# Attention and two gated layers on one core: two weight conversions at a time beside attention, two tiles split ahead, the first down products later

## The chip, the cores and the metric

The program runs on one core of one Trainium2 chip. The metric is the device time of one execution in microseconds; the kernel before takes 1159.92 us, the median of three runs (1158.78 to 1161.83).

## The reference, cut to what matters

Attention over 4 batches, 12 heads, 448 positions and a head width of 64 feeds two dense layers over 1792 tokens of width 768. The attention weight is a sigmoid, not a softmax.

```python
scores = q @ k.T / sqrt(64) - log(448);  x = sigmoid(scores) @ v      # per batch and head
h = x @ w_in;  y = (h * cos(h)) @ w_out                               # layer 1, 768 -> 2048 -> 768
z = (silu(y @ w_gate) * (y @ w_val)) @ w_out2                         # layer 2, 768 -> 1536 -> 768
```

q, k and v are 32-bit floats. The five weight matrices arrive as 64-bit floats, and have to be turned into 32-bit ones on the chip.

## The kernel before, in words

**Precision.** Every product is made of three passes over pairs of high and low parts of the operands (`THREE`, line 176). A tile is "split" when ScalarE has copied its high part and VectorE has subtracted that from the whole to get the low part; `split` and `lower` in `operands()` (lines 400 to 419) do this for weights. A split weight tile lives in one slot of `pairs`.

**Stages.** First `attention()` (line 511): 24 pairs of heads, one after the other. For each pair, TensorE makes the scores of three blocks of 128 keys (line 559), then the weighted sums of the pair before (lines 583 and 586), then the scores of the 64 keys left over (line 571). ScalarE makes the sigmoids (line 549) and copies the high part of the weighted sum (line 615); VectorE splits q and k of the next pair (lines 538 to 546) and takes the low part of the weighted sum (the `lo` of line 616, recorded at line 530). That low part reads PSUM bank 7, which the next pair's weighted sums write. Then layer 1: 8 chunks of the width 2048, each for 4 groups of 448 tokens, 32 units in all; a unit is two up products (`up`, 18 matmuls each, line 863) and three down steps (`down`, 12 matmuls each, line 720) that `some(downs)` runs one at a time. Then layer 2: two halves of the tokens, six chunks each, the up products in a seven-product scheme (`seven`, line 809).

**Weight conversion.** There are 68 tiles of 768 KB. `conversions()` (line 299) loads one, runs one or two ScalarE and four or five VectorE instructions over it, stores 384 KB to a scratch in DRAM, and takes the next. During attention four such chains run, on four pieces of the result buffers R[0] and R[1] that attention does not need (`lent`, lines 211 to 214). From the fourth last pair on (line 620) a chain that ends its tile takes no further one. After attention two chains run on buffers of their own, and share one slot for the converted tile (`convs`).

**Reading the weights back.** `loads()` (line 363) brings converted tiles in order of need into a ring of three slots, and `operands()` splits them as `pairs` slots come free. One `pairs` slot exists during attention (`make_pairs(xp, 1, "a")`, line 224), and four more are made after it (line 911).

**Order of the work.** All is written out by a planner (class `Order`): each task asks for an engine and names a time, the planner starts the earliest that can start, and the lower rank wins a tie (up products 0, h cos h 3, weight splits 4, conversions 6). The chip then keeps that order on each engine. In attention the planner is told with `beside(...)` (line 469) how much of each 6.0 us pair slot attention itself takes: ScalarE 1.1 us of the first 2.0 and 3.3 of the other 4.0, VectorE the first 2.8, and the DMA issue queue of SP the first 2.0. Conversions get what is left.

```python
for i in range(2):                                   # tensor_engine(), layer 1, unit n
    yield from up(n, i, upbanks[next(turn) % 4])
    for _ in range(1 + i):                           # one down step of unit n - 1, then two
        yield from some(downs)
```

Of the kernel before, what the change touches and what calls it, by code (L numbers as in the profile page):

```python
# [9 lines left out]
F32 = mybir.dt.float32  # L10
# [139 lines left out]
def block_kernel(  # L150
# [12 lines left out]
    P = 128  # L163
    B, NP, D, _, _, S = qk.shape
# [21 lines left out]
    xp = ctx.enter_context(tc.tile_pool(name="xp", bufs=1))  # L186
# [5 lines left out]
    R = [xp.tile([P, 2, KD, N], F32, tag=f"r{h}", name=f"r{h}") for h in range(NH)]  # L192
# [16 lines left out]
        free_t.give(ring[:, a])  # L209

    WT, lent = KD * P, []
    for i in range(4):
        part = R[i // 2].rearrange("p j k n -> p (j k n)")[:, i % 2 * 3 * WT:(i % 2 + 1) * 3 * WT]
        lent.append((part[:, :2 * WT].bitcast(I32).rearrange("p (n two) -> p n two", two=2), part[:, 2 * WT:]))
    zero = R[1].rearrange("p j k n -> p (j k n)")[:, -S:].bitcast(mybir.dt.bfloat16)[:, :S]
    nlog = xp.tile([P, 1], F32, tag="nlog", name="nlog")
    warm = xp.tile([P, 1], F32, tag="warm", name="warm")
    pairs, singles, gslots, tmps, downbanks = (Slots(order) for _ in range(5))

    def make_pairs(pool, n, name):  # L220
        for i in range(n):
            pairs.give(pool.tile([P, 2, 2, KH, P], F32R, tag=f"w{name}{i}", name=f"w{name}{i}"))

    make_pairs(xp, 1, "a")
    for i in range(2):
        downbanks.give(4 + 2 * i)
    upbanks = [Slots(order) for _ in range(4)]
# [135 lines left out]
    def loads():  # L363
        for need in needs():
            t = yield free_t
            for w, f, i, k in need:
                there, event = scratch[id(w), f + i]
                yield event
                there = scratch[id(w), f + i][0]
                if k is None:  # L370
                    yield move(t, there)
                else:
                    yield move(t[:, i * W:(i + 1) * W], there[:, k * W:(k + 1) * W])
            arrived = order.event()
            arrivals.append((t, arrived))
            if waiting_load:
                waiting_load.pop(0).set()
            order.spawn(landed(arrived), 0)
# [101 lines left out]
    def inputs(h):  # L480

        b11, b12, b21, b22 = (R[h][:, j, k * KH:(k + 1) * KH] for k in range(2) for j in range(2))
        make = {
            1: (b11, None), 2: (b21, None), 5: (b11, (b12, b11)), 6: (b11, (b22, b11)),
            7: (b12, (b22, b12)), 4: (b21, (b21, b11)), 3: (b22, None),
        }

        def to_hi(out, t):
            def do(engine):
                if engine == "ACT":  # L490
                    nc.scalar.activation(out=out, in_=t, func=AF.Copy)
                else:
                    nc.vector.tensor_copy(out, t)
            return {"ACT": 1.55, "DVE": 1.2}, do

        yield source[h]
        for i in ORDER:
            yield x_left[h - 1, i] if h else x_used[PLACES[i][0]]
            t, parts = make[i]
            if parts:  # L500
                yield vec(1.6, t, parts[0], parts[1], SUB)
            hi, lo = X[i][:, :, 0], X[i][:, :, 1]
            yield to_hi(hi, t)
            yield vec(1.6, lo, t, f32(hi), SUB)
            x_ready[h, i].set()
# [193 lines left out]
    def down(n):  # L699

        layer, g, c = units[n]

        def weights(e, i):
            return ("d", c, i) if layer == 1 else ("d", n, i, e // KH)

        for j in range(2 if layer == 2 else 1):
            for i in range(2):
                yield g_ready[n, i, j]
            for d in range(0, KD, 2):
                first = yield downbanks  # L710
                for e in range(d, d + 2):
                    for i in range(2):
                        yield made_event(weights(e, i))

                def do(_, first=first, d=d, j=j):
                    for e in range(d, d + 2):
                        for i in range(2):
                            w, g = operand(weights(e, i)), gs[n, i, j]
                            for m, p in THREE:
                                nc.tensor.matmul(  # L720
                                    banks[:, first + e - d, :N],
                                    lhsT=w[:, m, e % KH if layer == 2 else e, :], rhs=g[:, p],
                                    start=(i, m, p) == (0, 0, 0), stop=(i, m) == (1, 1),
                                )

                yield {"PE": 12 * PRODUCT}, do
                for e in range(d, d + 2):
                    for i in range(2):
                        if e == KD - 1 and g == G - 1 if layer == 1 else j and e % KH == KH - 1:
                            give(weights(e, i))  # L730
                        if e == KD - 1:
                            gslots.give(gs.pop((n, i, j)))
                order.spawn(accumulate(n, j, d, first), 2)
                yield None
# [105 lines left out]
    def some(downs):  # L840

        got = None
        while True:
            try:
                want = downs.send(got)
            except StopIteration:
                return False
            if want is None:
                return True
            got = yield want  # L850

    def up(n, i, bank):

        _, g, c = units[n]
        out = yield bank
        yield made_event(("u", c, i))
        cols = slice(g % 2 * N, (g % 2 + 1) * N)

        def do(_):
            w, x = operand(("u", c, i)), X1[g // 2]  # L860
            for k in range(KD):
                for m, p in THREE:
                    nc.tensor.matmul(  # L863
                        out, lhsT=w[:, m, k, :], rhs=x[:, k, p, cols],
                        start=(k, m, p) == (0, 0, 0), stop=(k, m) == (KD - 1, 1),
                    )

        yield {"PE": 18 * PRODUCT}, do
        if g == G - 1:
            give(("u", c, i))  # L870
        if c == NF1 // 2 - 1 and i == 1 and g % 2:
            x_used[g // 2].set()
        order.spawn(h_cos_h((n, i, 0), out, lambda: bank.give(out)), 3)

    def tensor_engine():
        turn = itertools.count()
        downs = (want for want in ())
        for n in range(n_units):
            if n < n_first:
                for i in range(2):  # L880
                    yield from up(n, i, upbanks[next(turn) % 4])
                    for _ in range(1 + i):
                        yield from some(downs)
            else:
                if n == n_first:
                    while (yield from some(downs)):
                        pass
                z = {}
                for u in range(2):
                    yield from seven(n, u, next(turn), z, downs)  # L890
            downs = down(n)
        while (yield from some(downs)):
            pass

    with tc.manual_schedule():
        nc.gpsimd.memset(nlog, -math.log(S))
        for h in range(NH):
            order.spawn(inputs(h), 3.5)
        order.spawn(loads(), 3)
        order.spawn(operands(), 4)  # L900
        for raw, t in lent:
            returned.append(order.event())
            order.spawn(conversions(raw, t, returned[-1]), 6)
        attention()
        with tc.tile_pool(name="mp", bufs=1) as mp:
            for i in range(2):
                raws.give(mp.tile([P, WT, 2], I32, tag=f"raw{i}", name=f"raw{i}"))
                order.spawn(conversions(), 6)
            sum_room.append(mp.tile([P, W], F32, tag="sum", name="sum"))
            convs.give(mp.tile([P, WT], F32, tag="cv", name="cv"))  # L910
            make_pairs(mp, 4, "b")
            for i in range(4):
                gslots.give(mp.tile([P, 2, N], F32R, tag=f"g{i}", name=f"g{i}"))
            for i in range(3):
                tmps.give(mp.tile([P, 2, N], F32, tag=f"u{i}", name=f"u{i}"))
            order.spawn(tensor_engine(), 0)
            order.run()
            assert not order.open
# [51 lines left out]
```

## Time and profile before

| | us |
|---|---|
| median of three runs | 1159.92 |
| the profiled execution | 1162.79 |
| its span, first to last instruction | 1161.0 |
| attention, to the first up product | 168.98 |
| layer 1, to the last up product's end | 168.98 to 632.3 |
| layer 2 | 649.3 to 1161 |

Engines are named PE (TensorE), PEld (its weight loads), DVE (VectorE), ACT (ScalarE), POOL (GpSimd) and SP (which only issues DMAs here). A timeline row gives start, length, engine, source line, operation, output and inputs, count, and in brackets how long the engine stood idle before it and what ended that. Many conversions and splits are issued by helpers, so they carry the lines 233 (ScalarE), 236 (VectorE) and 242 (DMA); the tile names tell them apart: `r` and `raw` are conversion buffers, `cv` is a converted tile, `sw..` is a scratch in DRAM, `t` is a ring slot, `wa` and `wb` are split weights, `x` is the attention output. With the clock, 1.00 stands for TensorE's full speed.

### The profile page before, as it was taken

To read this page: it belongs to the slowest core of one execution; us is meant where nothing else is said; L and a number is where in the kernel's file an instruction comes from. 1 tells how busy PE (TensorE), PEld (TensorE's weight loads), DVE (VectorE), ACT (ScalarE), POOL (GpSimd) and SP (SyncE) were. 2 spreads that over 40 slices of the span, in tenths; PEclk is the share of its full clock that TensorE was granted. 3 is DMA by queue.
4 is the path that set the end of the run, shared out by engine and by line. 5 is a ranking of instruction groups with operands and counts; after the bars stand their busy time and mean duration, and the time that the engine had idled before them with its cause. 6 is when DMAs were issued, how large, how long until landed. Compare 5 with 4: busy or idle time off the path is not lost. (4 is left out here: it accounts for less than half of the span.)

```text
span 1161.0 us, 14377 instructions
## 1 busy us (share of the span) xinstructions
PE 1122.1 (97%) x5531; PEld 966.0 (83%) x5531; DVE 821.9 (71%) x1165; ACT 555.2 (48%) x837; POOL 80.6 (7%) x68
## 2 busy tenths in 40 slices
PE   8999989999999999999999889999998999999998
PEld 4445548999999999999998779999997899999997
DVE  5777756668787777777787977687469765557654
ACT  6677755654444444444444546454334344333430
POOL 0000000000000000000000311021021111112100
PEclk9999999999999999999999989999998999999999
DMA  9999934443333434343422254432210421121102
GB/s 272 255 278 284 275 123 159 138 142 117 131 128 123 136 115 143 109 150 110 150 102 76 68 182 158 149 124 82 69 55 28 133 92 62 55 68 55 41 15 95
DMA packets 51908, 146.42 MB, mean 126 GB/s; under 512 B 5760, under 2 KB 21120, under 8 KB 51840
## 3 DMA queue, kind: packets, MB, share of 16 engines
q1 hardware_dynamic: 51696, 145.28, 39.0%
q8 instruction: 43, 0.70, 0.3%
q10 hardware_dynamic: 144, 0.23, 0.1%
q14 instruction: 25, 0.20, 0.1%
HBM read 113.25 MB, written 32.24 MB: 125 GB/s over the span
## 5 line engine op out<-in xcount | busy, mean ns | idle before, releaser
L720 PE MATMUL banks<-g,wb 128*128 128x448 f32 x1512 | 340.7, 369 | 6.5 <-ACT g L233 3.5
L720 PEld LDWEIGHTS banks<-g,wb 128*128 128x128 f32 x1512 | 284.9, 189 | 34.9 <-ACT g L233 4.7
L236 DVE TENSOR_TENSOR r<-banks,r 128x896 f32<-128x896 f32 x144 | 157.0, 1091 | 126.0 <-PE banks L720 125.8
L809 PE MATMUL banks<-x,wb 128*128 128x448 f32 x864 | 188.0, 366 | 10.0 <-DVE x L236 4.6
L809 PEld LDWEIGHTS banks<-x,wb 128*128 128x128 f32 x864 | 162.5, 189 | 25.0 <-DVE x L236 5.2
L863 PE MATMUL banks<-x,wb 128*128 128x448 f32 x864 | 183.1, 365 | 0.0
L863 PEld LDWEIGHTS banks<-x,wb 128*128 128x128 f32 x864 | 162.9, 188 | 13.2
L233 ACT ACTIVATE g<-u 128x448 fp32r<-128x448 f32 x104 | 60.0, 577 | 142.8 <-DVE u L236 133.2
L233 ACT ACTIVATE u<-u 128x448 f32<-128x448 f32 x148 | 84.9, 576 | 81.0 <-DVE u L645 54.3
L233 ACT ACTIVATE u<-banks 128x448 f32<-128x448 f32 x104 | 56.2, 541 | 108.7 <-PE banks L863 65.8
L236 DVE TENSOR_TENSOR u<-u,banks 128x448 f32<-128x448 f32 x124 | 76.3, 616 | 43.9 <-PE banks L809 34.8
L720 PE MATMUL banks<-g,wa 128*128 128x448 f32 x360 | 88.5, 369 | 0.0
L236 DVE TENSOR_TENSOR wb<-t,wb 128x768 fp32r<-128x768 f32 x72 | 68.9, 966 | 19.9 <-ACT wb L233 19.3
L233 ACT ACTIVATE wb<-t 128x768 fp32r<-128x768 f32 x72 | 59.8, 840 | 46.5 <-PE banks L809 12.8
L236 DVE TENSOR_TENSOR g<-u,g 128x448 fp32r<-128x448 f32 x104 | 68.4, 660 | 18.0 <-ACT g L233 18.0
L809 PE MATMUL banks<-x,x 128*128 128x448 f32 x315 | 73.8, 384 | 4.1 <-DVE x L236 3.7
L583 PE MATMUL banks<-a,vs 128*64 128x448 f32 x288 | 63.3, 577 | 10.8 <-DVE x L530 10.8
L720 PEld LDWEIGHTS banks<-g,wa 128*128 128x128 f32 x360 | 68.3, 190 | 6.3
L809 PEld LDWEIGHTS banks<-x,x 128*128 128x128 f32 x315 | 62.0, 199 | 12.1 <-DVE x L236 4.1
L549 ACT ACTIVATE a<-banks,nlog 128x896 f32<-128x896 f32 x72 | 67.4, 1008 | 7.0 <-PE banks L559 6.8
L645 DVE SCALAR_TENSOR_TENSOR u<-u 128x448 f32<-128x448 f32 x64 | 39.8, 622 | 35.8 <-ACT u L233 35.7
L389 POOL TENSOR_TENSOR sum<-t 128x384 f32<-128x384 f32 x14 | 17.0, 1214 | 674.7 <-PE banks L720 577.9
(87 smaller groups left out, 1286.9 us busy)
## 6 DMA issues: line engine op xcount, KB each, us to landing
raw<-in_w_out SPq DMA_DIRECT2D x20, 768.0 KB, 4.6
raw<-in_qk SPq DMA_DIRECT2D x47, 224.0 KB, 9.5
raw<-in_w_gate SPq DMA_DIRECT2D x12, 768.0 KB, 4.7
raw<-in_w_val SPq DMA_DIRECT2D x12, 768.0 KB, 4.5
vs<-in_v SPq DMA_DIRECT2D x24, 320.0 KB, 8.0
r<-in_w_in SPq DMA_DIRECT2D x10, 768.0 KB, 9.3
t<-swg SPq DMA_DIRECT2D x19, 384.0 KB, 3.2
t<-swv SPq DMA_DIRECT2D x17, 384.0 KB, 3.0
```

The lines of the kernel that those rows point to most:

```text
L233: return {"ACT": time}, lambda _: nc.scalar.activation(**kw)
L236: return {"DVE": time}, lambda _: nc.vector.tensor_tensor(out=out, in0=in0, in1=in1, op=op)
L389: on.tensor_tensor(out=out, in0=a, in1=b, op=op)
L549: nc.scalar.activation(out=a, in_=sc, func=AF.Sigmoid, bias=nlog, scale=1.0 / math.sqrt(D))
L583: nc.tensor.matmul(o[half], lhsT=vw[:, 2 * c + j], rhs=a[:, j], start=c == 0, stop=False)
L645: yield {"DVE": 0.65}, lambda _: nc.vector.scalar_tensor_tensor(out=f, in0=f, scalar=MAGIC, in1=u, op0=ALU.subtract, op1=ALU.subtract)
L720: nc.tensor.matmul(banks[:, first + e - d, :N], lhsT=w[:, m, e % KH if layer == 2 else e, :], rhs=g[:, p], start=(i, m, p) == (0, 0, 0), s ...
L809: nc.tensor.matmul(bank, lhsT=w[:, m, k, :], rhs=x[:, k, p, :], start=(k, m, p) == (0, 0, 0) and i in (1, 5), stop=(k, m) == (KH - 1, 1), ...
L863: nc.tensor.matmul(out, lhsT=w[:, m, k, :], rhs=x[:, k, p, cols], start=(k, m, p) == (0, 0, 0), stop=(k, m) == (KD - 1, 1),)
```

## The change

Four edits. The chains beside attention are two instead of four, both in R[0]. The constant `nlog` and the small `warm` tile move into the tail of R[1]. Two of the five `pairs` slots now exist during attention, and three are made after it, so that two weight tiles can be split early. And in layer 1, for the units 0 and 1, all down steps stand behind the second up product: unit 0's three down steps then come after both up products of unit 1, not one of them between the two.

```diff
-    for i in range(4):
+    for i in range(2):
         part = R[i // 2].rearrange("p j k n -> p (j k n)")[:, i % 2 * 3 * WT:(i % 2 + 1) * 3 * WT]
         lent.append((part[:, :2 * WT].bitcast(I32).rearrange("p (n two) -> p n two", two=2), part[:, 2 * WT:]))
-    zero = R[1].rearrange("p j k n -> p (j k n)")[:, -S:].bitcast(mybir.dt.bfloat16)[:, :S]
-    nlog = xp.tile([P, 1], F32, tag="nlog", name="nlog")
-    warm = xp.tile([P, 1], F32, tag="warm", name="warm")
+    last = R[1].rearrange("p j k n -> p (j k n)")
+    zero = last[:, -S:].bitcast(mybir.dt.bfloat16)[:, :S]
+    nlog, warm = last[:, -S - 1:-S], last[:, -S - 2:-S - 1]
...
-    make_pairs(xp, 1, "a")
+    make_pairs(xp, 2, "a")
...
-                    for _ in range(1 + i):
+                    for _ in range(((1, 2) if n > 1 else (0, 3))[i]):
                         yield from some(downs)
...
-            make_pairs(mp, 4, "b")
+            make_pairs(mp, 3, "b")
```

## Rows read from the trace of the kernel before

**Rows 1.** The page's first part: busy us, share of the span, instructions.
```profile
PE 1122.1 (97%) x5531; PEld 966.0 (83%) x5531; DVE 821.9 (71%) x1165; ACT 555.2 (48%) x837; POOL 80.6 (7%) x68
```

**Rows 2.** Windows: length, busy by engine (instructions), granted clock, DMA share, GB/s.
```profile
8.00:150.00 142.00, 133.92 (x758) 72.27 (x756) 106.96 (x228) 105.47 (x134) 0.00 (x0) 0.97 0.94 273
150.00:160.00 10.00, 7.80 (x39) 3.60 (x37) 8.11 (x16) 4.72 (x7) 0.00 (x0) 0.83 0.30 118
...
300.00:400.00 100.00, 100.00 (x491) 91.86 (x491) 76.19 (x105) 45.92 (x75) 0.00 (x0) 1.00 0.39 133
...
632.32:700.00 67.68, 57.46 (x254) 50.50 (x253) 56.01 (x65) 33.94 (x49) 14.20 (x9) 0.92 0.35 117
700.00:860.00 160.00, 159.71 (x786) 147.05 (x785) 116.18 (x150) 72.50 (x114) 26.91 (x22) 1.00 0.34 107
```

**Rows 3.** Timeline of PE in attention: start, length, work, idle before.
```profile
10.18 1.20 PE L571 MATMUL banks<-q,kb 128*128 128x448 f32 x3
...
69.00 1.10 PE L571 MATMUL banks<-q,kb 128*128 128x448 f32 x3
...
74.97 1.11 PE L571 MATMUL banks<-q,kb 128*128 128x448 f32 x3
...
81.30 3.50 PE L583 MATMUL banks<-a,vs 128*64 128x448 f32 x12 [2.43 <-DVE x L530]
...
85.72 1.27 PE L571 MATMUL banks<-q,kb 128*128 128x448 f32 x3
...
164.26 1.11 PE L571 MATMUL banks<-q,kb 128*128 128x448 f32 x3
```

**Rows 4.** Timeline of DVE just before that stall.
```profile
75.31 0.36 DVE L538 CAST k<-raw 128x384 fp32r<-128x384 f32 x1 [3.72 <-DMA raw<-in_qk]
...
78.89 1.82 DVE L320 SCALAR_TENSOR_TENSOR r<-r 128x768 int32<-128x768 int32 x2
80.63 0.62 DVE L530 TENSOR_TENSOR x<-banks,x 128x448 fp32r<-128x448 f32 x1
```

**Rows 5.** Waits of DVE (20 to 160 us) and of SP's queue (0 to 200): total, times, longest.
```profile
DVE k L538 <- DMA raw<-in_qk: 22.4, 8, 3.8
...
SPq L242 <- DVE r L236: 57.3, 12, 8.9
```

**Rows 6.** DMA issues up to 165 us: all traffic; one kind, KB each, median us to landing.
```profile
DMA packets 16139, 41.84 MB, mean 254 GB/s; under 512 B 1791, under 2 KB 7935, under 8 KB 16127
...
raw<-in_qk SPq DMA_DIRECT2D x47, 224.0 KB, 9.5
```

**Rows 7.** Groups up to 169 us, two steps of a conversion: busy, mean ns | idle before.
```profile
L236 DVE CUSTOM_DVE_ANT_0 r<-r 128x1536 uint16<-128x1536 uint16 x18 | 16.9, 953 | 0.1
...
L317 DVE TENSOR_SCALAR r<-r 128x768 int32<-128x768 int32 x18 | 9.8, 553 | 0.0
```

**Rows 8.** Timeline of PE at the start of layer 1.
```profile
168.98 4.16 PE L863 MATMUL banks<-x,wa 128*128 128x448 f32 x18
...
182.86 0.47 PE L720 MATMUL banks<-g,wb 128*128 128x448 f32 x1 [1.83 <-ACT g L233]
...
196.07 3.80 PE L863 MATMUL banks<-x,wa 128*128 128x448 f32 x18
...
210.78 3.80 PE L863 MATMUL banks<-x,wa 128*128 128x448 f32 x18
...
225.49 3.80 PE L863 MATMUL banks<-x,wb 128*128 128x448 f32 x18
```

**Rows 9.** Timeline of DVE there: the low part of unit 0's second operand.
```profile
183.51 0.62 DVE L236 TENSOR_TENSOR g<-u,g 128x448 fp32r<-128x448 f32 x1
```

**Rows 10.** Timeline of SP: stores of the conversions after attention, the last tiles' first load.
```profile
183.62 0.32 SPq L242 DMA_DIRECT2D swo<-cv  x1
...
790.84 0.32 SPq L242 DMA_DIRECT2D swd<-cv  x1
...
837.52 0.80 SPq L242 DMA_DIRECT2D raw<-swd  x2
```

## The prediction

> **What bounds the kernel now.** I read the page's shares first: TensorE is busy for 97% of the span [rows 1], so what can be won is idle or slow TensorE time, and the question is where it lies. The windows by stage answer that [rows 2]. Layer 1 between 300 and 400 us has TensorE busy for all of 100 us at full clock: nothing can be won there. From 700 to 860 us it idles for 0.3 us. Attention is different: 133.92 of 142 us and a clock of 0.97, and one stretch at its end, 150 to 160 us, has 7.80 of 10 us at 0.83. The entry to layer 2 (632 to 700 us) lacks 10.2 us of 67.68.
>
> The TensorE timeline gives the loss in attention exactly. One pair of heads takes 5.97 us where nothing disturbs it (69.00 to 74.97), and TensorE then has no gap. From pair 0 at 10.18 to pair 23 at 164.26 are 23 periods, 137.3 us at that pace; they took 154.1. So 16.8 us are lost, in a few lumps: the period from 74.97 to 85.72 alone lost 4.8 us, with a wait of 2.43 us for VectorE's `lo` and twelve slow matmuls behind it, 3.50 us long [rows 3].
>
> VectorE's timeline just before says why [rows 4]. It stood idle 3.72 us for the q and k load of the next pair, then split it, then ran conversion steps (L320, two in 1.82 us), and only then came to the `lo` at 80.63 that frees bank 7. VectorE keeps its written order, so a late load delays all of it. In the table of waits that load cost VectorE 22.4 us in 8 waits, 2.8 us each, at most 3.8, and the stores of the conversions held SP's queue for 57.3 us [rows 5]. The DMA list agrees: 41.84 MB moved before 165 us and a q or k load took 9.5 us to land [rows 6], at a DMA share of 0.94 with 273 GB/s [rows 2], so some 290 GB/s when full. All the traffic of attention is 144 us of a full DMA, beside TensorE's undisturbed 147: as a mean it just fits, in bunches of four conversion loads it does not.
>
> **The change part by part.**
>
> *Two chains for four.* How many tiles are converted beside attention? Now 18 [rows 7]: four chains fill the VectorE time that the planner leaves, 3.2 us of each 6.0 us slot. With two chains, the planner's own numbers set the cycle. A load issued at 2.95 us of a slot lands, by its 0.8 + 0.15 + 5.0, at 2.9 of the next; ScalarE has room at 5.3, the second ScalarE step comes at 1.35 of the third slot, VectorE's four steps (0.6, 0.6, 1.0, 1.0 and gaps of 0.15) run from 2.8 to 6.45, and the store waits until 2.0 of the fourth. That is three slots for each tile. The first load is at 6.0 us of planned time, the first two cycles are shorter, and the flag that ends a chain falls at 130: loads near 6, 22, 37, 55, 73, 91, 109 and 127, so 8 tiles, and for the second chain, which must share ScalarE's gaps, 7 or 8. I take 15.5, 2.5 fewer than now.
>
> What this frees: 2.5 times 1.18 MB of 41.84 (a load of 0.79 and a store of 0.39), less one more 0.39 MB read for the tile that is now split early: 39.3 MB, 135 us of a full DMA instead of 144. On VectorE 2.5 times 3.0 us (0.95 twice and 0.55 twice [rows 7]), less one low part of 0.95. Both are small as means. The bunch is what shrinks: with two loads fewer in flight, up to 1.57 MB fewer stand ahead of a q or k load, 5.4 us at 290 GB/s. If half of that is felt on average, 2.7 us, a mean wait of 2.8 us is nearly gone; the longest, 3.8, goes when all is felt. Bounds: nothing saved if VectorE's own load is the cause, all 16.8 if the late loads are; no loss, since both DMA and VectorE get less to do. The stalls that I can follow start with a load, so I stay nearer that end: two thirds, 11.2 us.
>
> The Trainium skill has a rule that speaks against this, in "DMA: Bandwidth & Descriptors", section "Where 436 GB/s comes from": between HBM and SBUF the HBM side binds, at about 358 GB/s for a core. By it, attention's traffic would be 117 us of a full DMA (an estimate from that page), so the DMA would have had room all along and fewer chains would buy little there. The trace differs: its 16 DMA engines were 0.94 busy at 273 GB/s, so here the row decides; what the sum would be if DMA traffic were not the cause is the first rival.
>
> *A second `pairs` slot during attention.* The second up tile's split, one pass of ScalarE and one of VectorE over a tile (0.95 us, if it takes as long as the pass in [rows 7]), moves before the end of attention, into the gaps just freed. TensorE shows no wait between the first and the second up product now, so nothing is won; uncovered it would cost those 0.95 us. The total stays at five slots, so the tiles behind it keep their pace; the ring slot of that tile comes free a little earlier.
>
> *The first unit's down steps behind both up products.* Layer 1's up products begin at 168.98; by 196.07 TensorE has done four of them and three down steps. A whole steady unit, two ups and three downs, takes 14.71 us (210.78 to 225.49); two more ups are 36 matmuls at 0.202, 7.3 us. So 27.1 us went by for 22.0 of work: 5.1 lost, 1.83 of it as the one wait shown, for unit 0's second operand [rows 8]. That operand's low part was ready at 183.51 + 0.62 = 184.13 [rows 9]. With four ups first, the down steps start at 168.98 + 14.6 = 183.6 or, the first up being 0.3 slow, 183.9, and their fourth to sixth matmul, which need this operand, run from 184.5 on. It just fits. The step moves 36 matmuls and the three ScalarE copies of its results by 3.6 us; it issues no DMA and passes nothing in SP's or POOL's queue, and the bank that the next up product needs was released long before. I take 4.5 saved; bounds 3 (the operand comes 2 us later, since h cos h shares ScalarE with three splits) and 5.1.
>
> *`nlog` and `warm` in R[1].* Read by the sigmoids; that corner is first overwritten by layer 1's sums, after attention. Zero.
>
> *What comes back later.* 2.5 more tiles are converted after attention. The 50 now done took 12.4 us each from the first store to the last, at 790.84 [rows 10]. The last store moves by 2.5 times 12.4, less the 15.7 saved: about 806. The cover is VectorE's free time, 24 to 27% up to 860 us, beside a TensorE that never waits there [rows 2]; bare, it would be 2.5 times 3.0, 7.5 us. The last tiles are first loaded back at 837.52 [rows 10], by then at 822: in time. Two ring slots and a temporary that the chains hand back come 15 us later; TensorE idles for 0.3 us from 700 to 860, for more than half of which it did without them [rows 2, 10]. Zero, with 3 us either way.
>
> *Sum.* 11.2 + 4.5 = 15.7 us. The profiled execution took 1162.79 us around a span of 1161.0, so it would be 1147.1; it lies 2.87 above the median of 1159.92, so the median would be **1144**.
>
> **The rivals.**
>
> *The conversions themselves, not the loads, hold VectorE.* By planned slot 21 four chains have stored 14 tiles, two chains would have 14 as well, so the pace per pair is nearly the same. For it: two L320 steps stand between the split and the `lo` [rows 4]. Against: VectorE idled 22.4 us for loads [rows 5], and without that idle it has room. Only the 4.5 stay: 1155.4.
>
> *All stalls go.* The longest wait, 3.8, is shorter than the 5.4 us of traffic removed. Then 16.8 + 5.1: 1138.
>
> *The entry to layer 2 takes it back.* There the planner sets conversions, splits and the inputs of the seven products against each other, and all arrive at another phase. The loss there now is 10.2 us of idle time and, at a clock of 0.92, a sixth of 67.7 us at half speed, 5.4 more [rows 2]. Were it doubled, 15.6 go: 1160. Against: nothing in the order of these tasks changes, only their offset.
>
> *Starved by conversions: slower.* The last store precedes the first load of these tiles by 46.7 us, 3.8 conversions at 12.4 [rows 10]. From the fourth tile fewer on, each costs up to 12.4 us. If a chain took three and a half slots for a tile, 12 in all, 6 fewer, then 6 times 12.4 = 74.4, less 46.7: 27.7 us lost against 15.7 saved, 1172. Against: the planner's order is fixed and gives three slots, and the load stands somewhat ahead of need.
>
> **How the numbers follow.** Forecast 0.56 (its own range 1140 to 1149); VectorE the holder 0.15; all stalls gone 0.13; taken back at layer 2 0.09; starved 0.07. Within 0.3%, 3.5 us, a measurement cannot tell this kernel from no change. A quarter of the first rival falls within that, and so does the case taken back: 0.13 for the same; 0.07 slower; the rest, 0.80, faster. The range 1137 to 1157 leaves out the last two cases, 0.16.
>
> **What would show it.** Right, if the first up product starts near 158 instead of 168.98, q and k loads land in some 7 us and VectorE's wait for them falls below 8 us; if 15 or 16 conversions write to R[0]; if the fourth up product is followed by 36 down matmuls with under 1 us of idle time; if the last `swd` store comes near 806 and 700 to 860 stays full. Wrong, if attention's lumps stay with the loads in time (the first rival), if the window after layer 1 loses over 16 us, or if fewer than 13 tiles are converted beside attention.

## The result, and the profile after

The changed kernel takes 1146.07 us in the median of 16 runs (1143.57 to 1157.76), the kernel before 1159.72 in 16 runs beside it. The ratio is 0.989, with a 95% interval of 0.987 to 0.991: 13.7 us faster, where 1144 was forecast. The profiled execution of the changed kernel is its slowest one, 1157.76 us around a span of 1155.9, against 1162.79 before. So its stages must be read one by one.

The page's shares say that TensorE has the same 1122.1 us of work as in [rows 1], and VectorE 807.5 us, 14 less.

The windows of after (columns as in [rows 2]) show where it went. Attention has TensorE busy for 135.87 of 142 us instead of 133.92, at a clock of 1.00 instead of 0.97, with the DMA at 0.91 and 254 GB/s instead of 0.94 and 273. The gap at attention's end is gone, and the stretch behind layer 2's entry is still full:

```profile
8.00:150.00 142.00, 135.87 (x793) 74.63 (x793) 106.72 (x221) 110.92 (x141) 0.00 (x0) 1.00 0.91 254
150.00:160.00 10.00, 9.31 (x50) 4.49 (x47) 0.76 (x2) 4.58 (x7) 0.00 (x0) 1.00 0.01 2
...
690.00:850.00 160.00, 160.00 (x791) 148.27 (x790) 120.72 (x163) 78.80 (x121) 27.94 (x25) 1.00 0.40 135
```

The timeline of TensorE answers to [rows 3] and [rows 8]. From pair 0 to pair 23 it now takes 144.25 us instead of 154.08. What is left of the waits for `lo` is 0.76 us and the like, and the twelve matmuls behind take 2.48 us, not 3.50. Layer 1 begins at 159.09 instead of 168.98, with four up products in a row and 36 down matmuls behind them, without a gap:

```profile
10.12 0.88 PE L571 MATMUL banks<-q,kb 128*128 128x448 f32 x3
...
101.82 2.48 PE L583 MATMUL banks<-a,vs 128*64 128x448 f32 x12 [0.76 <-DVE x L530]
...
154.37 1.12 PE L571 MATMUL banks<-q,kb 128*128 128x448 f32 x3
...
159.09 15.38 PE L863 MATMUL banks<-x,wa 128*128 128x448 f32 x72
174.31 7.60 PE L720 MATMUL banks<-g,wb 128*128 128x448 f32 x36
```

In VectorE's waits (20 to 160 us, as [rows 5]) the loads of q and k no longer come first. They cost it 6.0 us instead of 22.4; ScalarE's step in a conversion costs it 11.7 instead of 0.5. (Its largest wait, 17.3 us in 9, is for ScalarE's copy of the weighted sum, which was 9.8 in 8 before.)

```profile
DVE r L314 <- ACT r L292: 11.7, 10, 2.3
DVE k L538 <- DMA raw<-in_qk: 6.0, 4, 2.0
```

Fourteen tiles are converted beside attention, not 18 [rows 7] and not the forecast 15.5:

```profile
L236 DVE CUSTOM_DVE_ANT_0 r<-r 128x1536 uint16<-128x1536 uint16 x14 | 13.4, 957 | 0.5
```

So 54 are left for later. SP's timeline (as [rows 10]) shows the 41st of these stores and the last one, which comes at 859.56, not at 790.84; the first load of that tile into the ring follows 2.3 us later, so it had to wait for the store. At the entry to layer 2's second half TensorE waits for 8.63 us, where before it waited 3.72:

```profile
664.75 0.32 SPq L242 DMA_DIRECT2D swd<-cv  x1
...
859.56 0.32 SPq L242 DMA_DIRECT2D swd<-cv  x1
861.88 0.32 SPq L242 DMA_DIRECT2D t<-swd  x1
```

```profile
887.59 5.97 PE L809 MATMUL banks<-x,x 128*128 128x448 f32 x15 [8.63 <-DVE x L236]
```

The same by stages, measured between the starts of matmuls in the two traces, in us. Attention runs from pair 0's row to the first up product, the first two units from there to unit 2's first; the rest of layer 1 is taken from unit 4's first up product to the last one, the entry to layer 2 from there to the 631st product of line 809, the second half's entry from the 757th to the 883rd, and the last row is all the rest of layer 2:

| | before | after | of the change |
|---|---|---|---|
| attention | 158.80 | 148.97 | -9.8 |
| first two units | 27.09 | 22.66 | -4.4 |
| units 2 and 3 | 29.41 | 29.76 | +0.3 |
| rest of layer 1 | 403.19 | 407.96 | +4.8 |
| entry to layer 2 | 219.1 | 218.8 | -0.3 |
| second half's entry | 49.57 | 51.84 | +2.3 |
| rest of layer 2 | 263.6 | 265.8 | +2.2 |

Three things in this table were not in the prediction: layer 1, which was to be untouched, is 4.8 us longer, and so are the second half's entry, by 2.3, and the rest of layer 2, by 2.2. In sum this execution is only 5 us shorter than the profiled one of before, where the medians differ by 13.7; e1 and the experiments on `nlog` and `warm` below bear on that.

### The profile page after: what moved, and what is told of

Its sections match the earlier page's. It is cut to its first block, busy times and chain, and to the rows that moved or that the text cites. A ratio compares the mean times of both kernels' runs of the same rounds, so it can differ in the third digit from the quotient of the medians.

```text
span 1155.9 us, 14399 instructions
## 1 busy us (share of the span) xinstructions
PE 1122.1 (97%) x5531; PEld 964.1 (83%) x5531; DVE 807.5 (70%) x1143; ACT 573.1 (50%) x858; POOL 80.1 (7%) x69
## 4 chain that ended last, share of the span: by engine, by line
PE 89%; DVE 5%; DMA 4%; ACT 1%; issue 1%; SPq 0%; ACTq 0%; DVEq 0%
PE banks L720 35%; PE banks L809 27%; PE banks L863 21%; DMA raw<-in_qk 3%; PE banks L583 3%; PE banks L559 2%; PE banks L586 1%; DVE x L236 1%; DVE r L236 1%; DMA vs<-in_v 1%; DMA r<-in_w_out 1%; PE banks L571 1%; ACT a L549 0%; DVE r L320 0%; DVE x L530 0%
## 5 line engine op out<-in xcount | busy, mean ns | idle before, releaser
L720 PE MATMUL banks<-g,wb 128*128 128x448 f32 x1080 | 244.5, 368 | 1.2 <-DVE g L236 1.1
L720 PEld LDWEIGHTS banks<-g,wb 128*128 128x128 f32 x1080 | 202.8, 188 | 21.3 <-DVE g L236 1.4
L720 PE MATMUL banks<-g,wa 128*128 128x448 f32 x792 | 181.6, 368 | 1.7 <-DVE g L236 1.4
L720 PEld LDWEIGHTS banks<-g,wa 128*128 128x128 f32 x792 | 148.5, 188 | 16.7 <-DVE g L236 1.8
L809 PE MATMUL banks<-x,wb 128*128 128x448 f32 x666 | 149.5, 373 | 8.2 <-DVE x L236 5.4
L809 PEld LDWEIGHTS banks<-x,wb 128*128 128x128 f32 x666 | 127.0, 191 | 21.3 <-DVE x L236 6.5
L863 PE MATMUL banks<-x,wb 128*128 128x448 f32 x648 | 139.7, 368 | 0.0
L863 PEld LDWEIGHTS banks<-x,wb 128*128 128x128 f32 x648 | 121.6, 188 | 12.3
L863 PE MATMUL banks<-x,wa 128*128 128x448 f32 x504 | 108.5, 369 | 0.0
L863 PEld LDWEIGHTS banks<-x,wa 128*128 128x128 f32 x504 | 94.6, 188 | 9.9 <-issue 0.4
L809 PE MATMUL banks<-x,wa 128*128 128x448 f32 x432 | 94.7, 366 | 0.7 <-ACT banks L233 0.7
L809 PEld LDWEIGHTS banks<-x,wa 128*128 128x128 f32 x432 | 81.0, 188 | 8.0 <-ACT banks L233 1.1
L809 PEld LDWEIGHTS banks<-x,x 128*128 128x128 f32 x315 | 61.9, 198 | 15.6 <-DVE x L236 9.0
L549 ACT ACTIVATE a<-banks,r 128x896 f32<-128x896 f32 x72 | 67.2, 1003 | 7.2 <-PE banks L559 7.1
```

Of the source, the lines that this page charges most:

```text
L549: nc.scalar.activation(out=a, in_=sc, func=AF.Sigmoid, bias=nlog, scale=1.0 / math.sqrt(D))
L720: nc.tensor.matmul(banks[:, first + e - d, :N], lhsT=w[:, m, e % KH if layer == 2 else e, :], rhs=g[:, p], start=(i, m, p) == (0, 0, 0), s ...
L809: nc.tensor.matmul(bank, lhsT=w[:, m, k, :], rhs=x[:, k, p, :], start=(k, m, p) == (0, 0, 0) and i in (1, 5), stop=(k, m) == (KH - 1, 1), ...
L863: nc.tensor.matmul(out, lhsT=w[:, m, k, :], rhs=x[:, k, p, cols], start=(k, m, p) == (0, 0, 0), stop=(k, m) == (KD - 1, 1),)
```

## Experiments

Medians are given beside the median of before in the same batch (1160.8 for the first four, 1160.7 for e4, e9, e12 and e10, 1158.7 for the rest), and the ratio with its 95% interval.

**e1: the changed kernel again,** for its spread.

> The changed kernel once more, nothing edited, for a second profile. In the first profile an up product of layer 1 takes 3.72 us (3.64 before) and TensorE waits 8.6 us at the entry to the second half of layer 2. If the first comes from where the tiles lie, it is 3.72 here too; if it is a matter of the run, it may be 3.64, and this run then ends some 4 to 5 us sooner. If the late last conversions cause the 8.6 us, the wait is here too (6 to 9 us), and the last conversion is stored near 860. Attention should again end near 159.

1146.07 us, ratio 0.991 [0.988, 0.994]. The runs fall in two groups: seven from 1143.3 to 1146.3 and five from 1154.5 to 1158.6. The profiled one, 1157.37, is of the upper group, and its rest of layer 1 takes 407.96 us as in the first profile. Attention takes 148.06. After's own 16 runs do the same, with five from 1150.8 to 1157.8. So the upper group is no accident of one run, and attention, as short as in e2's profile (148.33), isn't its cause.

**e2: two chains alone.**

```diff
-    for i in range(4):
+    for i in range(2):
```

> The kernel before with two chains for four and nothing else (15 tiles converted beside attention). My theory, bunched conversion loads hold up the q and k loads: the first up product starts near 159 instead of 169, VectorE's wait for q and k loads falls below 10 us, the start of layer 1 still loses 5 us, about 1150 in all. Rival, the conversions' own VectorE time holds up the low part: the pace of conversions is nearly the same, so the first up product stays at 166 or later, about 1157.

1153.12 us, 0.994 [0.992, 0.996]: 7.7 us. Attention takes 148.33 us, with 15 tiles, and VectorE waits for no load of q or k from 20 to 160 us. The first two units stay at 27.0 and the rest of layer 1 at 403.20; the last store comes at 820.6.

**e3: the down steps alone.**

```diff
-                    for _ in range(1 + i):
+                    for _ in range(((1, 2) if n > 1 else (0, 3))[i]):
```

> The kernel before with the first unit's down steps behind both up products and nothing else. From the first up product to the start of unit 2's first up product 22.7 us instead of 27.1, so 4.4 saved, about 1155.3; attention as before, near 169. If the saving is taken back at the entry to layer 2, the time is 1159 to 1160.

1152.22 us, 0.993 [0.990, 0.996]: 8.6 us, nearly twice what the step can give. The first two units take 22.35 us, 4.7 less, as forecast. A second part lies at the second half's entry: 48.49 us here and 48.50 to 48.82 in e7, e9 and e12, which have the step too, against 49.57 to 51.14 in before, e10, e2 and e5, which haven't. The rest of this profile's gain lies in attention, 152.24 us, though its written order is that of before (158.80 there); the profile is of the fastest of e3's eight runs. So one profile of an attention with 18 tiles says little to within 6 us.

**e5: four chains, but the loads of q and k three pairs ahead instead of two,** to take away the late load and leave the conversions.

```diff
-                raw = at.tile([P, 2, S], F32, tag="raw", name=f"raw{i}", bufs=3)
-                vs = at.tile([P, 2 * NCH * D + 2 * P], F32, tag="vs", name=f"vs{i}", bufs=4)
+                raw = at.tile([P, 2, S], F32, tag="raw", name=f"raw{i}", bufs=4)
+                vs = at.tile([P, 2 * NCH * D + 2 * P], F32, tag="vs", name=f"vs{i}", bufs=5)
...
+            load(2, (nc.sync, nc.sync))
...
-                if i + 2 < NPAIR:
-                    load(i + 2, (nc.sync, nc.sync))
+                if i + 3 < NPAIR:
+                    load(i + 3, (nc.sync, nc.sync))
```

> The kernel before, four chains and 18 tiles as before, but attention loads q, k and v three pairs ahead instead of two (one more buffer of each kind). My theory: VectorE's wait for these loads, 28 us, falls below 8, and the first up product comes near 159, 10 us sooner, with no fewer conversions; 1149 or so in all. Rival, VectorE's own conversion work: the waits go, but TensorE's waits for the low part stay, and the first up product is at 166 or later, 1157 to 1160.

1152.98 us, 0.994 [0.992, 0.996]: 7.7 us, as much as two chains give, with all 18 tiles. VectorE's wait for loads from 20 to 160 us is gone. But attention's 152.54 us are 4 more than with two chains in e2's profile. TensorE's waits there (columns: total, times, longest) still have long ones:

```profile
PE banks L583 <- DVE x L530: 6.5, 4, 2.8
```

VectorE waits for ScalarE's conversion step in this kernel for up to 4.7 us. So the late load is a cause, and in this execution the conversions are one of their own. But it is the slowest of e5's 12 runs, 1159.50 us, 6.5 above the median, and e2's profile is of its median run; whether a usual run of e5 has these 4 us is not shown.

**e10: before again.**

> The kernel before once more, nothing edited, for a second profile. In the first, attention ran to 168.98; the same instruction order in attention ran to 162.40 with the later down steps. If that difference is a matter of the run, attention ends between 160 and 168 here, and the 16.8 us that the forecast counted as lost were those of a slow run; typical would be 10 to 13.

1161.71 us, 1.001 [0.998, 1.003]; attention 157.48, VectorE's wait for loads 24.8 us in 10. The lumps of before are no accident: from pair 0 to pair 23 15.4 us are lost, where I thought 10 to 13 typical.

**e9: two chains and the down order,** nothing else.

> The changed kernel without its early pair: two chains and the later down steps, but one pairs slot during attention and nlog and warm as tiles of their own. Two questions. The times of the changed kernel fall in two heaps, near 1144.5 and near 1156, and in both its profiles successive matmuls of layer 1 come 206.7 ns apart instead of 202. If the placing of the tiles causes that, this kernel has only the lower heap (all runs 1142 to 1149) and an up product of 3.64 us in its profile; if any kernel of this speed can fall into it, both heaps are there. And if the early pair is worth nothing, the median is that of the lower heap, near 1145.

1145.17 us, 0.987 [0.985, 0.990]: 15.5 us, where e2 and e3 alone make 16.2. The two edits add up, and they are the whole gain. Fifteen tiles; the last store at 841.8; TensorE's wait at the second half's entry 5.5 us.

**e12: e9 with the loads three ahead** (the edit of e5).

> The kernel of e9_chains_and_order, with attention's q, k and v loaded three pairs ahead instead of two. My theory, late loads stall attention: with two chains little of that is left, so this gives at most 2 us over e9 (VectorE's wait for loads, about 7 us with two chains, below 5; first up product at 157 or sooner). Rival, VectorE's conversion steps cause what is left: no difference to e9.

1146.99 us, 0.988 [0.986, 0.991]: no more to gain from loads once there are two chains. Its attention takes 151.18 us, 2.6 of them in one wait for `lo` at the start, at 20.84.

**e4: before with only the early pair and the corner of R[1].**

```diff
-    nlog = xp.tile([P, 1], F32, tag="nlog", name="nlog")
-    warm = xp.tile([P, 1], F32, tag="warm", name="warm")
+    nlog, warm = last[:, -S - 1:-S], last[:, -S - 2:-S - 1]
...
-    make_pairs(xp, 1, "a")
+    make_pairs(xp, 2, "a")
...
-            make_pairs(mp, 4, "b")
+            make_pairs(mp, 3, "b")
```

> The kernel before with two pairs slots during attention and nlog and warm in R[1], nothing else (four chains, 19 tiles converted beside attention). The forecast put this edit at nothing: 1160, within 3 us. If the placing of the tiles sets the matmuls' pace, an up product of layer 1 takes 3.72 us in its profile and part of the runs are 5 to 11 us slower, the median 1160 to 1170.

1155.72 us, 0.998 [0.995, 1.001], with nine runs from 1153.0 to 1157.3 and three from 1163.4 to 1169.9. The interval includes no change; the three long runs pull the ratio up, for the medians alone lie 4.9 us apart. In the profile, which is of the fastest run, the rest of layer 1 took 400.06 us, so these two edits can move TensorE's pace in both directions. The first two units took 24.34 us, where the four kernels with neither the pair nor the down order (before, e10, e2, e5) take 27.00 to 28.36.

**e13: the changed kernel with `nlog` and `warm` as tiles of their own again,** and **e14: e9 with these two in R[1],** to tell the early pair from the corner.

```diff
# e13, against after
-    nlog, warm = last[:, -S - 1:-S], last[:, -S - 2:-S - 1]
+    nlog = xp.tile([P, 1], F32, tag="nlog", name="nlog")
+    warm = xp.tile([P, 1], F32, tag="warm", name="warm")
# e14: the reverse edit, against e9
```

> The changed kernel with nlog and warm as tiles of their own again, as before the change; the early pair stays (14 tiles converted beside attention). If those small tiles, by shifting all that is placed after them, set the matmuls' pace, layer 1's matmuls come 202 ns (ups) and 206.5 ns (downs) apart here, the long stretch of layer 1 takes 403.2 us, and all runs lie in one heap near 1147. If the second early pair is the cause, the two heaps of the changed kernel are still there, near 1144.5 and 1156.

> The kernel of e9_chains_and_order (one early pair) with nlog and warm moved into the corner of R[1], nothing else. If moving them sets the pace, ups and downs of layer 1 both come 202.7 ns apart in some runs and 206.7 in others, the long stretch of layer 1 takes 400 or 408 us, and the times fall in two heaps near 1141 and 1153. If the second early pair is the cause, one heap near 1145, as e9.

e13: 1147.96 us, 0.991 [0.989, 0.993], six runs within 2.5 us of each other, none in an upper group. e14: 1143.09 us, 0.988 [0.985, 0.990], one of six at 1148.45. It has the lowest median of all kernels here, but its batch was faster as a whole, and its ratio is that of e9. The groups by line from 300 to 600 us (matmuls, busy us, mean ns of one) of after, e13 and e14, in this order, show what the corner does:

```profile
L863 PE MATMUL banks<-x,wb 128*128 128x448 f32 x440 | 95.0, 368 | 0.0
```

```profile
L863 PE MATMUL banks<-x,wb 128*128 128x448 f32 x451 | 95.3, 364 | 0.0
```

```profile
L863 PE MATMUL banks<-x,wb 128*128 128x448 f32 x594 | 125.7, 365 | 0.0
```

At the same granted clock of 1.00 and with no idle time, one up matmul is 364 ns long with own tiles, 368 in after's profile, and 365 in e14. From start to start these are 202.1, 206.7 and 202.7 ns; down matmuls go at 206.5 with own tiles and at the pace of the ups in the other two. Nor does the place of the tiles alone set the pace. From 700 to 850 us, in layer 2, after has come down to the pace of e14, and e1, the same kernel, has not (after first):

```profile
L809 PE MATMUL banks<-x,wb 128*128 128x448 f32 x225 | 48.8, 365 | 0.0
```

```profile
L809 PE MATMUL banks<-x,wb 128*128 128x448 f32 x225 | 49.7, 369 | 0.0
```

**e7: e9 with three chains,** and **e8: e9 with one.**

```diff
-    for i in range(2):
+    for i in range(3):    # e7;  range(1) in e8
```

> The kernel of e9_chains_and_order with three chains instead of two; 19 tiles are converted beside attention, one more than four chains manage in the kernel before. My theory, loads in flight together hold up q and k: attention lies between two chains (148) and four (157), near 151; the wait at the entry to layer 2's second half is 3.7 us again, as the conversions end early; about 1147. Rival, the number of conversions in attention, so their VectorE work: attention is as slow as with four, 155 or more, and the time 1151 or more.

> The kernel of e9_chains_and_order with one chain instead of two; 8 tiles are converted beside attention instead of 15. Attention about 147, 1 us sooner. The forecast's slower rival, starvation: the last conversion is stored some 7 times 12.9 = 90 us later, near 930, after the point where TensorE needs it; TensorE waits in layer 2's first half, and the time is 1190 to 1230. If conversions fill idle VectorE time as fast as wanted, the time stays within 5 us of e9.

e7: 1150.58 us, 0.993 [0.991, 0.996]. Three chains convert 19 tiles, one more than four do, and attention takes 157.77 us, as before, in a profile of the slowest of its six runs. The window and VectorE's waits for loads (20 to 160 us) have the full DMA and the late loads back:

```profile
8.00:150.00 142.00, 131.81 (x742) 70.50 (x741) 110.14 (x227) 108.46 (x139) 0.00 (x0) 0.96 0.97 284
```

```profile
DVE k L538 <- DMA raw<-in_qk: 18.0, 9, 2.9
```

This fell against my theory that the number of loads in flight counts: three lies halfway between two and four, and gained nothing. The medians say the same: the ratio is that of e3, 0.993, where the down order stands alone with four chains. What three and four chains share is the tiles through attention.

e8: 1175.97 us, 1.015 [1.013, 1.018]. Eight tiles are converted beside attention, which takes 148.28 us, no less than with 15. The last store comes at 887.7, not near 930, and in layer 2 TensorE waits for split weights, once for 15.71 us:

```profile
856.89 1.11 PE L809 MATMUL banks<-x,wb 128*128 128x448 f32 x2 [15.71 <-ACT wb L233]
```

So starving is real, though milder than I priced it, 12.4 us a tile: e8 is 17.3 us above its before and e9 15.5 below, which makes 33 us for seven tiles fewer, 4.7 each.

## Why the prediction came out, step by step

**Attention, forecast 11.2 us: right in place, too large in size.** From pair 0 to pair 23, 9.8 us came back of the 16.8 lost, but before's profiled run is 3 us above its median; by medians e2 gave 7.7, and its interval, 4.8 to 8.9 us, leaves 11.2 out. The theory was that late loads start the stalls. e5 bears it out by taking the lateness away with all four chains left: 7.7 us too, with as many tiles, as much traffic and as many conversion steps as before. e5's profile, of its slowest run, also shows the first rival at work, for its attention is 4 us longer than e2's; how much of that a usual run has is open. With two chains no wait for `lo` in e2 is longer than 0.8 us, and e12 finds nothing left for the loads. A long wait cost more than itself: behind the three of 1.9 to 2.4 us in before, the granted clock fell to 0.50 for 3.4 us, and the twelve matmuls there took 3.50 to 4.17 us instead of 2.48; behind after's waits, 0.98 us at most, it stayed at 1.00. The 7 us that after still loses are waits of 0.6 to 1.0 us, mostly in every third pair. VectorE's timeline before the one at 101.82 has them: it waits for ScalarE's step of a conversion, runs its four steps, and only then the `lo`:

```profile
98.09 0.56 DVE L314 TENSOR_SCALAR r<-r 128x768 f32<-128x768 f32 x1 [2.24 <-ACT r L292]
...
101.15 0.61 DVE L530 TENSOR_TENSOR x<-banks,x 128x448 fp32r<-128x448 f32 x1
```

**Why fewer chains helped, forecast as a smaller bunch and a shorter landing: only half right.** The argument of 1.57 MB less in flight would have given three chains about half of the gain; e7 gave none. Nor is a shorter landing what the kernels with two chains share: from issue to landing the loads of q and k took 8.6 us on the mean in e2 and 8.5 in after, and 8.4 to 8.9 in before, e10, e3 and e7 (7.1 to 7.6 in e1, e9, e13 and e14). What they share is an earlier issue. Over pairs 4 to 23, a pair's first load was issued 7.8 us ahead of the line-571 products of the pair two before it in before, e10 and e3, 7.4 in e7 and 6.9 in e4; with two chains (after, e1, e2, e9, e13 and e14) it was 8.9 to 9.5. SP's waits in e2 (0 to 200 us, as [rows 5]) show how the queue that issues them has changed:

```profile
SPq L524 <- PE banks L586: 47.3, 19, 4.6
SPq L242 <- DVE r L236: 40.3, 14, 8.4
```

Before, stores waiting for VectorE's conversions held this queue for 57.3 us [rows 5] (54.5 in e7), and the loads stood behind them. In e2 they hold it for 40.3, and it waits longest for TensorE to release a `vs` buffer, 47.3 us instead of 15.5: the queue is ahead of its buffers. e5 wins the same time by asking three pairs ahead. The traffic sorts the profiles too: with 18 and 19 tiles the DMA moves 273 to 284 GB/s in the window from 8 to 150 us and attention takes 152 to 159 us; with 14 and 15 it is 254 to 257 GB/s and 148 to 149 us (151 in e12); 8 tiles, at 199 GB/s, bring no less. But e5 gains as much by its median at 279 GB/s, so traffic alone doesn't cost the time. That the held queue makes the loads late is likely and not shown, since stores, traffic and conversions all go with the tiles.

After's DMA list up to 155 us has 37.52 MB, and a load landed in 8.6 us in the median, not 7 (6.9 in e9):

```profile
DMA packets 15132, 37.52 MB, mean 242 GB/s; under 512 B 1680, under 2 KB 7824, under 8 KB 15120
...
raw<-in_qk SPq DMA_DIRECT2D x47, 224.0 KB, 8.6
```

The Trainium skill's rule weighed there ("DMA: Bandwidth & Descriptors", section "Where 436 GB/s comes from", some 358 GB/s) was set aside for 290 GB/s when full. e7's 284 GB/s at a share of 0.97 makes it 293, so the trace differs from the rule again.

**Tiles, forecast 15.5: 14.** The planner's cycle of three slots was right, e2 and e9 have 15. The missed term is the early pair: with it, after and e13 have 14. That its splits and the extra read take a place from the chains is argued only, for with four chains e4 has 19, one more than before.

**The down order, forecast 4.5: 4.4** in the profiles (27.09 to 22.66), and 4.7 in e3. The fourth to sixth matmul found their operand ready, as the 36 in one row show. By medians e3 gave 8.6, with an interval of 4.8 to 11.4 us: the step is worth more than the stretch that it was priced on, some 1 to 2.7 us of it at the second half's entry, and why it acts there is open.

**The early pair, forecast 0: not seen as a gain beside the down order.** Alone with the corner, in e4's profile, it shortened the first two units by some 3 us, a loss that the down order takes away without it (22.35 in e9, 22.21 in e13). e13 is e9 with the pair, and its ratio is 0.991 [0.989, 0.993] against 0.987 [0.985, 0.990]. With the tile that is missing, the second half's wait is 8.6 us instead of 5.5.

**`nlog` and `warm`, forecast "Zero": the step that failed.** I looked only for a conflict in time over that corner, and I had said of layer 1, full at full clock, that nothing can be won there. In every profiled kernel with own tiles the rest of layer 1 took 403.2 us; with the two in R[1] it took 400.06 (e4, e14) or 407.96 (after, e1). That is -3.1 or +4.8 us in this stage alone. The profiles of after and e1 are both of the upper group of runs, at 1157 us, and those of e4 and e14 are of the fastest runs of their kernels; e13, the same as after but for this edit, had none above 1148.3 in six. From the first up product to the last the two paces make 8.9 us (460.4 in after, 451.5 in e14), and the medians of e1's two groups lie 11.3 apart. It is likely that the pace parts the groups, but no run of the lower group of after or e1 was profiled, so that isn't shown. Why the place of two small tiles changes the pace, and why one kernel has two, even within one execution, is open.

**Later, forecast last store 806, cost 0: the store was wrong by 54 us, the cost by some 2.** I took the mean of 12.4 us for a conversion. From the trace it is 11.77 us in the steady part of layer 1 and 13.5 in layer 2 (668.99 to 790.84 for nine). In after the last thirteen took 15.0 each, 664.75 to 859.56. It is 13.5 in e2, 15.6 in e3 and 15.0 to 15.3 in e9, e13 and e14, so the new down order goes with the slower rate; but e4 has 14.6 without it, and why is open. So four tiles more moved the last store by 69 us: four at 15.0, nine at 1.5 us more each, less 4.2 for the earlier start. The last store then stands right ahead of its load. TensorE's wait there is 3.7 us in the seven profiles whose last store comes by 821, 5.5 in the three with 836 to 844 (e9, e12, e14) and 8.6 in the three with 854 to 860 (e13, after, e1), so the reserve seems to end about there. The stage itself grew less, from 49.57 to 51.84 us, with 48.51 in e9; before has 49.6 and 51.0 in two profiles, so these 2 us are no more than likely. The rival "taken back at layer 2" is refuted at the place that it named: that entry is 219.1 before and 218.8 after.

So the sum, 15.7, came near 13.7 in part by luck. Its two large terms were right in place. But by medians the chains gave 7.7 for a forecast of 11.2 and the down order 8.6 for 4.5, and these misses cancel. Perhaps 2 us at the second half, and a term of either sign in the pace, were not in it.

## What to carry to other kernels

Where side work shares the DMA and the elementwise engines with a stage that is just covered, give it less than the mean allows: here, in the profiles, three tiles more cost attention 4 to 10 us, and the tiles left out were nearly free until their reserve ran out. Or issue the stage's own loads earlier: by medians e5 gained as much with all the tiles. Read that reserve at the late stage's own rate, not at the mean over all stages. Try the parts of a change alone, and repeat the kernel before: two of the four edits made this gain, and single profiles of one stage spread by 6 us. A profile shows one run: know where that lies among the kernel's runs.

## What the runs showed of the hardware

TensorE's pace in a full stretch at a granted clock of 1.00 was not one number: 202.1 or 206.5 ns from start to start with own tiles, by the line, and 202.7 or 206.7 for all lines with two tiles of one column each placed elsewhere. After's profile has both: 206.7 from 300 to 600 us and 202.7 from 700 to 850, with the tiles where they were. Attention with the written order of before took 152.2 to 158.8 us in three profiles (before, e10, e3) at 273 to 279 GB/s, and with two chains 148.0 to 149.0 in the six of after, e1, e2, e9, e13 and e14 at 254 to 257.
